# Causal scores in 64-key halves, and value products in two halves of queries, in a gated-attention and FFN kernel

## The chip, the cores and the metric

The kernel runs on one core of one Trainium2 chip. The metric is the device time of one execution in microseconds (us). Before the change the median of three runs is 655.03 us (653.73 to 656.40). The execution that was profiled took 653.01 us; its span, from its first to its last instruction, is 651.2 us.

## The reference, cut to what matters

There are 4 sequences, 8 heads, 768 steps and a head dimension of 48. Per head a complex state is decayed element by element and updated at each step, and only its real part is read:

```
S_re, S_im = a_re*S_re - a_im*S_im + k v^T,  a_re*S_im + a_im*S_re     # |a| capped at 0.999
y[t] = q[t] @ S_re
```

The 8 heads' outputs side by side give x, 3072 x 384. Then h = x @ w_in (384 x 2048), g = h * cos(h), and the result is g @ w_out (2048 x 384). All data is float32 (the weights arrive as float64).

## The kernel before, in words

**Chunks.** Time is cut into chunks of C = 128 steps: 24 chunks n in all, 6 to a sequence, handled in 12 groups g of G = 2 chunks. For a chunk the recurrence becomes a causal attention within the chunk plus a term from the state at its start. With the decay folded into queries and keys, both have 2 x 48 = 96 rows (real and imaginary part).

**Scores.** `f_scores(n, hh)` (line 958) does four heads (HH = 4, hh = 0 or 1): for each a matmul with the 128 keys as weights and the 128 queries as moving columns, contraction over 96 rows, into the PSUM tile `sc`. Then one VectorE multiply by the constant mask `causal` (0.25 on and above the diagonal, 0 below it) moves 128 x 512 numbers into the SBUF tile `atm`. Keys lie on the partitions, so a quarter of each 128 x 128 square (keys 64 to 127 against queries 0 to 63) is computed and then multiplied by 0.

**Values.** `f_out(n)` (line 970) makes the output transposed, dimension by step, in the PSUM tile `yp`. Two heads share a PSUM column block: the even head's 48 rows start at partition 0, the odd head's at partition 64 (`side`). For each pair p of heads it issues the two sides' products of values with `atm` (contraction over 128 keys, weights of 48 columns, 128 moving columns) and, unless the chunk is a sequence's first, the two sides' products of `state` with the queries (contraction over 96 rows, 48 weight columns, 128 moving columns), which add to the same place. ScalarE then copies both halves out.

**State.** `f_state(n)` (tile `sp`) multiplies keys and values for the next chunk's state, except in a sequence's last chunk.

**FFN.** `mm1` (tile `hp`) multiplies x by w_in; ScalarE and VectorE make g of it. From group 2 on the second product is done in seven instead of eight block products (`seventh`, tiles `sum` and `op`, moving 192 columns), issued in half-products of 8 matmul records.

A float32 matmul appears in the trace as two MATMUL records, each with its own LDWEIGHTS: 192 score products are 384 records.

**What sets the order.** All TensorE instructions go through `matmul` (line 687), which chains each one behind the one before. GpSimd's instructions are chained in the same way (`chain(..., "gpsimd")`, lines 549, 629, 1279); VectorE's ordinary ones go through `vector` (line 676) and are ordered by the framework from group 2 on. From there `weave` (line 1213) writes the order: each list of steps is spread over a stretch of the group's unit interval and all are sorted. In group n the `chunks(n)` steps (scores hh = 0, scores hh = 1, state, output, for both chunks) lie in 0.0 to 0.36, between half-products of the group before; the FFN's first product comes from 0.56 on.

**Groups 0 and 1** (chunks 0 to 3) have an order written by hand and use other forms in part (`f_rows` for chunks 0 and 1). PEG = 2 is the first group of the regular kind, so 20 of the 24 chunks are regular.

**GpSimd** does little: it issues the DMAs of constants and raw weights. In groups 4 to 11 `guarded` (line 1281) gives it one tiny copy that waits for a gate tile and then two DMAs of raw weights (tile `raw`, one buffer at that stage), whose exponents VectorE and ScalarE check.

Of the kernel before, what the change touches and what calls it, by code (L numbers as in the profile page):

```python
# [11 lines left out]
F32 = mybir.dt.float32  # L12
# [7 lines left out]
ALU = mybir.AluOpType  # L20
# [467 lines left out]
def fast_path(ctx, tc, q, k, v, a_re, a_im, moe_w_in, moe_w_out, out, least, odd, wide,  # L488
# [7 lines left out]
    nc = tc.nc  # L496
    B, H, S, D = q.shape
    DM, DF = moe_w_in.shape
    C = 128
    NCH = S // C  # L500
    G = 2
    N = B * NCH
    NG = N // G
    D2 = 2 * D
    HH = H // 2
    ND = DM // C
    Q4 = C // 32
# [6 lines left out]
    ld = ctx.enter_context(tc.tile_pool(name="ld", bufs=1))  # L514
    gt = ctx.enter_context(tc.tile_pool(name="gt", bufs=1))
    ft = ctx.enter_context(tc.tile_pool(name="ft", bufs=2))
# [4 lines left out]
    stage = {"pool": room.enter_context(tc.tile_pool(name="stage", bufs=1)), "bufs": 4}  # L521
    pa = ctx.enter_context(tc.tile_pool(name="pa", bufs=5, space=PSUM))
# [3 lines left out]
    causal_np = (step_np[:, None] <= step_np[None, :]).astype(np.float32)  # L526
# [10 lines left out]
    def chain(ins, engine="scalar"):  # L537

        if engine in tail:
            behind(ins, tail[engine])  # L540
        tail[engine] = ins

    def behind(ins, other):
        tc.add_manual_dep(ins.ins, other.ins.name, mybir.DependencyInfo(
            mybir.DependencyClass.NoSync, mybir.DependencyReason.DATA))

    def constant(array, name, queue=None, pool=consts):
        t = pool.tile(list(array.shape), F32, name=name)
        put = (queue or nc.gpsimd).dma_start(
            out=t, in_=nc.inline_tensor(array, name=name + "_const").ap())  # L550
        if queue is None:
            chain(put, "gpsimd")
        return t
# [6 lines left out]
    X = [dict() for _ in range(NG)]  # L560
    Y = [dict() for _ in range(N)]
# [3 lines left out]
    PEG, PER = 2, 1  # L565
# [118 lines left out]
    vector, scalar = Ordered(nc.vector, "vector"), Ordered(nc.scalar, "scalar")  # L684

    def matmul(out, **kw):
        chain(nc.tensor.matmul(out, **kw), "tensor")  # L687
# [156 lines left out]
    def p_even(g, i, n):  # L844
        for _ in even_steps(g, i, n):
            pass
# [8 lines left out]
    def p_apply(g, i, n):  # L855
        x = X[g]
        P, Q, u = (cut(x[name], i, n) for name in ("P", "Q", "mag"))
        vector.tensor_tensor(out=Q, in0=cut(x["k"], i, n), in1=Q, op=ALU.mult)
        vector.tensor_tensor(out=u, in0=cut(x["q"], i, n), in1=P, op=ALU.mult)

    def g_angle(g, i, n):

        at = cut(X[g]["tan"], i, n)
        special(out=at, in_=at, func=AF.Arctan)
# [4 lines left out]
    def g_carry(g):  # L869

        n, some = g * G, ds(C - 32, 32)
        if g >= PEG and n % NCH:
            head = cut(X[g]["tan"], 0, 1)[some]
            X[g]["carried"] = vector.scalar_tensor_tensor(
                out=head, in0=before(n)[some], scalar=carry[some], in1=head,
                op0=ALU.mult, op1=ALU.add)

    def g_split(g):
        if g >= PEG:
            X[g]["split"] = upper_half(g, cut(X[g]["tan"], 0, G), 1.0 / math.pi)()  # L880
# [71 lines left out]
    def queries(n, h):  # L952
        g, i = divmod(n, G)
        if g < PEG:
            return X[g]["qT"][:, i * H + h].rearrange("p q j -> p (q j)")
        return X[g]["qT"][:, :, i * H + h]

    def f_scores(n, hh):
        y = Y[n]
        if hh == 0:  # L960
            y["atm"] = ft.tile([C, H, C], F32, tag="atm", name="atm")
        ps = pa.tile([C, HH, C], F32, tag="a", name="sc")
        for h in range(HH):
            head = hh * HH + h
            matmul(ps[:, h], lhsT=X[n // G]["kT"][:, n % G * H + head],
                   rhs=queries(n, head), start=True, stop=True)
        y["masked"] = vector.tensor_tensor(
            out=y["atm"][:, ts(hh, HH)], in0=ps, in1=causal.unsqueeze(1).to_broadcast([C, HH, C]), op=ALU.mult)

    def f_out(n):  # L970
        y, (g, i) = Y[n], divmod(n, G)
        vals = X[g]["v"][:, i]
        state = y.get("state")
        if i == 0:
            X[g]["yT"] = ft.tile([C, HH, G, C], F32, tag="yT", name="yT", bufs=1)
        ps = pa.tile([C, HH, C], F32, tag="a", name="yp")
        for p in range(HH):
            for side in range(2):
                matmul(ps[ds(side * 64, D), p], lhsT=vals[:, 2 * p + side],
                       rhs=y["atm"][:, 2 * p + side], start=True, stop=(state is None))  # L980
            if state is not None:
                for side in range(2):
                    matmul(ps[ds(side * 64, D), p], lhsT=state[:, 2 * p + side],
                           rhs=queries(n, 2 * p + side), start=False, stop=True)
        for side in range(2):
            half = ds(side * 64, D)
            scalar.copy(out=X[g]["yT"][half, :, i], in_=ps[half])

    def f_rows(n, lo=0, hi=H):

        y, (g, i) = Y[n], divmod(n, G)
        state = y.get("state")
        if lo == 0:
            y["yr"] = pa.tile([C, H, D], F32, tag="a", name="yr")
        ps = y["yr"]
        for h in range(lo, hi):
            matmul(ps[:, h], lhsT=y["atm"][:, h], rhs=X[g]["v"][:, i, h],
                   start=True, stop=(state is None))
            if state is not None:
                matmul(ps[:, h], lhsT=queries(n, h), rhs=state[:, h], start=False, stop=True)  # L1000
        if hi < H:
            return
        y["rows"] = msb.tile([C, DM], F32, tag="ot", name="rows")
        scalar.copy(out=y["rows"], in_=ps.rearrange("p h d -> p (h d)"))
# [74 lines left out]
    def gate_sine(g, jp):  # L1079
        x = X[g]  # L1080
        ps = x["hp"][jp]
        gate = x["gate"][jp] = msb.tile([C, 2, G * C], F32, tag="gate", name="gate", bufs=8)
        junk = msb.tile([C, 2, G * C], BF16, tag="junk", name="junk", bufs=1)
        special(out=gate, in_=ps, func=AF.Sin, scale=1.0 / in_scale, bias=half_pi_b)
        scalar.activation(out=junk, in_=ps, func=AF.Square, scale=1.0 / in_scale,
                          accum_out=wide[:, ds(g * (NJ // 2) + jp, 1)])

    def gate_product(g, jp):
        x = X[g]
        gate = x["gate"][jp]  # L1090
        gated = vector.tensor_tensor(out=gate, in0=x["hp"].pop(jp), in1=gate, op=ALU.mult)
        x.setdefault("gated", gated)

    def mm1_gate(g, jp):
        gate_sine(g, jp)
        gate_product(g, jp)
# [143 lines left out]
    def powers(g):  # L1240
        return [lambda i=i: p_powers(g, i) for i in range(G)]

    def prods(g):
        if not 0 <= g < NG:
            return
        if g not in (1, 2):
            yield from powers(g)
            yield lambda: g_angle(g, 0, G)
        yield lambda: (g_carry(g), g_split(g))
        yield lambda: (p_even(g, 0, G), p_apply(g, 0, G))  # L1250
# [23 lines left out]
    def second(g, i):  # L1274
        return [lambda j0=j0: mm2(g, i, j0, 4) for j0 in range(0, NJ, 4)] if g < PLAIN else []
# [26 lines left out]
    chain(nc.gpsimd.tensor_copy(out=alls, in_=one_b.to_broadcast([C, C])), "gpsimd")  # L1302
    parts = into + back
    pieces = [weight(dst, src) for dst, src in parts[:2]]
    causal = constant(causal_np * np.float32(0.25), "causal")
    pieces += [weight(dst, src) for dst, src in parts[2:RAW]]
    carry = constant(carry_np, "carry")
    chain(nc.gpsimd.tensor_copy(out=exact, in_=ones), "gpsimd")
# [3 lines left out]
    one, two = (log_steps(0, i, 1) for i in range(2))  # L1312
# [93 lines left out]
    state = state_next(1)  # L1406
# [55 lines left out]
    state = state_next(2)  # L1462
# [12 lines left out]
    state = state_next(3)  # L1475
# [86 lines left out]
    Ordered.by_hand, Ordered.mark = (), dict(tail)  # L1562
    for jp in 6, 7:
        mm1_gate(1, jp)
    room.close()
    stage.update(pool=ctx.enter_context(tc.tile_pool(name="late", bufs=1)), bufs=1)
    quarters()
    for n in range(2, NG):
        weave((mixes(n - 1, 2, 4), 0.0, 0.12), (logs(n + 1), 0.0, 0.02), (chunks(n), 0.0, 0.36),
              (upper[2:] if n == 2 else [], 0.0, 0.2), (products(n - 1, 0, 2 + (n < NG - 1)), 0.0, 0.36),  # L1570
              (prods(n + 1), 0.25, 0.27), (second(n - 1, 1), 0.36, 0.5),
              (products(n - 1, 2 + (n < NG - 1), 7), 0.4, 0.56),
              (phases(n + 1), *((0.472, 0.476) if n == PLAIN else (0.516, 0.524))),
              (keys(n + 1), *((0.5, 0.62) if n == PLAIN else (0.53, 0.64))),
              (last_quarter() if n == PLAIN else [], 0.9, 1.0), (first(n), 0.56, 1.0),
              (mixes(n, 0, 2), 0.9, 1.0), (guarded(n - 1, per) if n > 3 else [], 0.1, 0.9))
# [101 lines left out]
```

## Time and profile before

| what | value |
|---|---|
| median of 3 runs | 655.03 us |
| profiled execution | 653.01 us, span 651.2 us, granted TensorE clock 1.000 |
| `sc` MATMUL records | 384, of them 320 in regular chunks |
| `yp` MATMUL records from `atm` / from `state` | 352 / 304 |
| `atm` multiplies on VectorE | 48 x 689 ns |
| GpSimd busy | 30.9 us in 53 instructions |

An engine's busy time counts a stretch once, however many of its instructions overlap there. Since matmuls are pipelined, a group's mean duration (276 ns for `sc`) is not what one more of them costs; the distance from start to start is. In the timeline, consecutive instructions of one form are merged into one row with its count, start and length.

### The profile page before, as it was taken

The numbers are of one execution on the slowest core, as the hardware profiler recorded it, in microseconds if no ns is written. First come the engines' busy times: TensorE is split into PE (matmuls) and PEld (weight loads), VectorE is DVE, ScalarE is ACT, GpSimd is POOL, SyncE is SP. The second block draws the span as 40 slices with busy tenths as digits, with TensorE's granted clock in tenths as the row PEclk, the third lists the DMA queues.
The fourth block names the chain that finished last, engine by engine and source line by source line (L and its number), as shares of the span: only waits on it lengthen the run. The fifth ranks groups of instructions, "written<-read, shape, count | busy, mean of one in ns | idle before, by whom it ended". The sixth has DMA issues, their size and how long they took to land.

```text
span 651.2 us, 10758 instructions
## 1 busy us (share of the span) xinstructions
PE 641.0 (98%) x4075; PEld 576.4 (89%) x4075; DVE 492.0 (76%) x799; ACT 392.8 (60%) x726; POOL 30.9 (5%) x53
## 2 busy tenths in 40 slices
PE   8999999999999999999999999999999999999997
PEld 6888877777999999899899899899899999999996
DVE  6999989888687688786787787876877878862251
ACT  7898687284583593494494485485576476433330
POOL 4010200000000000010010010000000000000000
PEclk9999999999999999999999999999999999999999
DMA  9968755727627656747738737836836843363001
GB/s 249 244 179 203 225 164 123 170 62 182 146 49 182 158 146 148 194 110 167 209 82 191 204 85 167 205 96 151 226 105 146 219 123 98 112 134 120 25 1 31
DMA packets 232920, 94.90 MB, mean 146 GB/s; under 512 B 208701, under 2 KB 221246, under 8 KB 232858
## 3 DMA queue, kind: packets, MB, share of 16 engines
q1 hardware_dynamic: 225320, 68.51, 45.3%
q0 software_dynamic: 5824, 25.50, 11.7%
q8 instruction: 34, 0.56, 0.4%
q10 hardware_dynamic: 1714, 0.11, 0.2%
q14 instruction: 28, 0.23, 0.1%
HBM read 69.28 MB, written 24.81 MB: 144 GB/s over the span
## 4 chain that ended last, share of the span: by engine, by line
PE 92%; ACT 4%; DVE 3%; DMA 0%; issue 0%; SPq 0%; DVEq 0%
PE hp L687 38%; PE op L687 18%; PE sum L687 16%; PE sc L687 6%; PE yp L687 6%; PE sp L687 4%; PE phs L687 2%; PE lgs L687 1%; ACT tan L707 1%; PE yr L687 1%; PE tp L948 1%; ACT rs L707 1%; ACT lg L707 1%; ACT L703 1%; DVE mag L676 1%; DVE atm L676 1%
## 5 line engine op out<-in xcount | busy, mean ns | idle before, releaser
L687 PE MATMUL hp<-xT,w_in 128*128 128x256 f32 (+1 forms) x1176 | 252.5, 375 | 0.0
L687 PEld LDWEIGHTS hp<-xT,w_in 128*128 128x128 f32 x1176 | 219.6, 190 | 30.2 <-issue 0.2
L707 ACT ACTIVATE gate<-hp,half_pi_b 128x512 f32<-128x512 f32 x96 | 66.0, 687 | 118.5 <-PE hp L687 118.5
L687 PE MATMUL op<-w_out,gate 128*128 128x192 f32 (+1 forms) x448 | 100.7, 374 | 0.0
L676 DVE TENSOR_TENSOR gate<-hp,gate 128x512 f32<-128x512 f32 x96 | 65.7, 684 | 45.8 <-ACT junk L676 45.7
L687 PEld LDWEIGHTS op<-w_out,gate 128*128 128x128 f32 x448 | 75.9, 190 | 16.9 <-issue 2.0
L676 ACT ACTIVATE junk<-hp 128x512 bf16<-128x512 f32 x96 | 56.7, 591 | 0.0
L687 PE MATMUL sum<-t_s,s 128*128 128x192 f32 x320 | 56.3, 329 | 0.0
L687 PEld LDWEIGHTS sum<-t_s,s 128*128 128x128 f32 x320 | 52.1, 190 | 1.5 <-issue 1.5
L676 DVE TENSOR_TENSOR atm<-sc,causal 128x512 f32<-128x512 f32 x48 | 32.9, 689 | 23.4 <-PE sc L687 23.4
L687 PEld LDWEIGHTS sc<-qT,kT 96*128 96x128 f32 x384 | 47.4, 192 | 2.3 <-issue 0.6
L687 PE MATMUL sc<-qT,kT 96*128 96x128 f32 x384 | 49.0, 276 | 0.2 <-ACT qT L676 0.2
L676 ACT ACTIVATE ot<-sum 128x192 f32<-128x192 f32 x39 | 12.6, 322 | 53.7 <-PE sum L687 53.4
L676 DVE SCALAR_TENSOR_TENSOR ot<-op,ot 128x192 f32<-128x192 f32 x40 | 13.3, 354 | 38.0 <-PE op L687 36.4
L687 PE MATMUL yp<-atm,v 128*48 128x128 f32 x352 | 33.6, 277 | 0.9 <-ACT Q L707 0.6
L703 ACT ACT_TABLE_LOAD x24 | 30.8, 1283 | 1.2 <-PEq L1662 0.7
L676 ACT COPY yT<-yp 48x512 f32<-48x512 f32 x44 | 25.3, 574 | 7.4 <-PE yp L687 7.0
L687 PE MATMUL yp<-qT,state 96*48 96x128 f32 x304 | 29.7, 272 | 0.0
L687 PE MATMUL sum<-w_out,gate 128*128 128x192 f32 x160 | 29.7, 329 | 0.0
L687 PE MATMUL sp<-v,ks 128*96 128x48 f32 x320 | 29.7, 245 | 0.0
L687 PEld LDWEIGHTS sp<-v,ks 128*96 128x96 f32 x320 | 29.6, 165 | 0.0
L676 ACT CAST tan<-phs 128x384 int32<-128x384 f32 x24 | 11.4, 480 | 29.4 <-PE phs L687 29.4
(147 smaller groups left out, 987.4 us busy)
## 6 DMA issues: line engine op xcount, KB each, us to landing
moved<-tr SPq DMA_DIRECT2D x20, 768.0 KB
raw<-in_moe_w_in_dram POOLq DMA_DIRECT2D x16, 768.0 KB, 5.1
raw<-in_moe_w_out_dram POOLq DMA_DIRECT2D x16, 768.0 KB, 4.6
kT<-moved SPq DMA_DIRECT2D x40, 192.0 KB
qT<-moved SPq DMA_DIRECT2D x10, 768.0 KB
k<-in_k_dram SPq DMA_DIRECT2D x24, 192.0 KB
q<-in_q_dram SPq DMA_DIRECT2D x24, 192.0 KB
v<-in_v_dram SPq DMA_DIRECT2D x24, 192.0 KB
```

The costliest lines, as they stand in the source:

```text
L676: ins = getattr(self.engine, op)(**kw)
L687: chain(nc.tensor.matmul(out, **kw), "tensor")
L703: chain(nc.scalar.preload_act_table_set(table))
L707: chain(nc.scalar.activation(func=func, **kw))
L948: chain(nc.tensor.transpose(ps[:, h], X[g][name[0] + "s"][:, x0 + h].rearrange("p a d -> p (a d)"), ident), "tensor")
```

## The change: what it does

In chunks 4 to 23 `f_scores` becomes `half_scores` and the products with `atm` in `f_out` become `half_out`; a new `swap_values` serves them.

- `half_scores` cuts the keys into two halves of 64, so that the weights have 64 columns. The first half is multiplied with all 128 queries, the second only with queries 64 to 127. The even head's first half goes to partitions 0 to 63, the odd head's to 64 to 127; the second halves go to the opposite side. A pair of heads thus fills three blocks of 64 columns instead of four, with four products instead of two, and the mask multiply moves 128 x 384 instead of 128 x 512.
- `half_out` issues the state products first, then the values in two halves of queries: for queries 0 to 63 only the 64 first keys count, so the contraction is over 64 rows (partitions 0 to 63 for the even head, 64 to 127 for the odd one); for queries 64 to 127 it is over 128. Each has 64 moving columns.
- In the odd head's last block the key halves lie swapped, so its values must too: `swap_values` makes, with two GpSimd copies per group, a tile `odd` of the odd heads' values with halves of partitions exchanged. It has one buffer and is issued in the weave of the group before, at 0.4 to 0.42.
- A mask `halves_mask` is loaded as one more constant; `causal` and part of the first groups' `atm` move to a pool that is released later.

```diff
+    def swap_values(g):
+        odd_v = X[g]["odd"] = ld.tile([C, G, HH, D], F32, tag="odd", name="odd_v", bufs=1)
+        for lo in 0, C // 2:
+            src = X[g]["v"][ds(C // 2 - lo, C // 2)].rearrange("p g (x two) d -> p g x two d", two=2)
+            chain(nc.gpsimd.tensor_copy(out=odd_v[ds(lo, C // 2)], in_=src[:, :, :, 1]), "gpsimd")
+    def half_scores(n, hh):
+        y, (g, i), S = Y[n], divmod(n, G), C // 2
+        if hh == 0:
+            y["atm"] = ft.tile([C, HH, 3, S], F32, tag="atm", name="atm")
+        ps = pa.tile([C, HH // 2, 3, S], F32, tag="a", name="sc")
+        keys = X[g]["kT"].rearrange("d x q j -> d x (q j)")
+        for p in range(HH // 2):
+            heads = [i * H + hh * HH + 2 * p + side for side in range(2)]
+            for side, head in enumerate(heads):
+                matmul(ps[ds(side * S, S), p, ds(0, 2, 1 + side)], lhsT=keys[:, head, 0:S],
+                       rhs=X[g]["qT"][:, :, head], start=True, stop=True)
+            for side, head in (1, heads[1]), (0, heads[0]):
+                matmul(ps[ds((1 - side) * S, S), p, 1 + side], lhsT=keys[:, head, S:C],
+                       rhs=X[g]["qT"][:, Q4 // 2:Q4, head], start=True, stop=True)
+        y["masked"] = vector.tensor_tensor(
+            out=y["atm"][:, ts(hh, HH // 2)], in0=ps,
+            in1=halves_mask.unsqueeze(1).to_broadcast([C, HH // 2, 3, S]), op=ALU.mult)
+    def half_out(n, ps):
+        y, (g, i), S = Y[n], divmod(n, G), C // 2
+        state = y.get("state")
+        for p in range(HH):
+            vals = X[g]["v"][:, i, 2 * p], X[g]["odd"][:, i, p]
+            if state is not None:
+                for side in range(2):
+                    matmul(ps[ds(side * 64, D), p], lhsT=state[:, 2 * p + side],
+                           rhs=queries(n, 2 * p + side), start=True, stop=False,
+                           skip_group_check=True)
+            for half in range(2):
+                for side in range(2):
+                    rows = ds(0, C) if half else ds(side * S, S)
+                    matmul(ps[ds(side * 64, D), p, ts(half, S)], lhsT=vals[side][rows],
+                           rhs=y["atm"][rows, p, half * (1 + side)], start=(state is None),
+                           stop=True, skip_group_check=True)
     def f_scores(n, hh):
+        if n >= PEG * G:
+            return half_scores(n, hh)
...
-        for p in range(HH):
+        if g >= PEG:
+            half_out(n, ps)
+        for p in range(HH if g < PEG else 0):
...
-    causal = constant(causal_np * np.float32(0.25), "causal")
+    causal = constant(causal_np * np.float32(0.25), "causal", pool=stage["pool"])
+    S = C // 2
+    halves_np = np.stack([np.tile(causal_np[:S, :S], (2, 1)), causal_np[:, S:],
+                          np.roll(causal_np[:, S:], S, axis=0)], axis=1) * np.float32(0.25)
+    halves_mask = constant(halves_np, "halves_mask")
...
+    swap_values(PEG)
...
+              ([lambda: swap_values(n + 1)] if n + 1 < NG else [], 0.4, 0.42), (second(n - 1, 1), 0.36, 0.5),
```

More of the change, by code (lines that the diff above doesn't have):

```diff
@@ L958, in f_scores @@
     def f_scores(n, hh):
+        if n >= PEG * G:
+            return half_scores(n, hh)
         y = Y[n]
-        if hh == 0:
-            y["atm"] = ft.tile([C, H, C], F32, tag="atm", name="atm")
+        pool = stage["pool"] if hh else ft
+        atm = pool.tile([C, HH, C], F32, tag="atm", name="atm", bufs=2)
+        y.setdefault("atm", []).append(atm)
         ps = pa.tile([C, HH, C], F32, tag="a", name="sc")
@@ L967, in f_scores @@
         y["masked"] = vector.tensor_tensor(
-            out=y["atm"][:, ts(hh, HH)], in0=ps, in1=causal.unsqueeze(1).to_broadcast([C, HH, C]), op=ALU.mult)
+            out=atm, in0=ps, in1=causal.unsqueeze(1).to_broadcast([C, HH, C]), op=ALU.mult)
     def f_out(n):
@@ L976, in f_out @@
         ps = pa.tile([C, HH, C], F32, tag="a", name="yp")
-        for p in range(HH):
+        if g >= PEG:
+            half_out(n, ps)
+        for p in range(HH if g < PEG else 0):
             for side in range(2):
                 matmul(ps[ds(side * 64, D), p], lhsT=vals[:, 2 * p + side],
-                       rhs=y["atm"][:, 2 * p + side], start=True, stop=(state is None))
+                       rhs=y["atm"][p // 2][:, p % 2 * 2 + side], start=True, stop=(state is None))
             if state is not None:
@@ L996, in f_rows @@
         for h in range(lo, hi):
-            matmul(ps[:, h], lhsT=y["atm"][:, h], rhs=X[g]["v"][:, i, h],
+            matmul(ps[:, h], lhsT=y["atm"][h // HH][:, h % HH], rhs=X[g]["v"][:, i, h],
                    start=True, stop=(state is None))
@@ L1570, in fast_path @@
               (upper[2:] if n == 2 else [], 0.0, 0.2), (products(n - 1, 0, 2 + (n < NG - 1)), 0.0, 0.36),
-              (prods(n + 1), 0.25, 0.27), (second(n - 1, 1), 0.36, 0.5),
+              (prods(n + 1), 0.25, 0.27),
+              ([lambda: swap_values(n + 1)] if n + 1 < NG else [], 0.4, 0.42), (second(n - 1, 1), 0.36, 0.5),
               (products(n - 1, 2 + (n < NG - 1), 7), 0.4, 0.56),
```

## Prediction

> **What bounds the kernel now.** I read the page's busy shares first, then the chain that ended last, then TensorE's timeline for one group.
>
> ```profile
> PE 641.0 (98%) x4075; PEld 576.4 (89%) x4075; DVE 492.0 (76%) x799; ACT 392.8 (60%) x726; POOL 30.9 (5%) x53
> ...
> PE 92%; ACT 4%; DVE 3%; DMA 0%; issue 0%; SPq 0%; DVEq 0%
> ```
>
> TensorE is busy in 98% of the span and makes 92% of the chain. In the regular part it hardly idles: the table by stretches shows 51.00 us busy of 51.00 between 204 and 255 us. So what the change adds to or takes from TensorE's start-to-start distances goes into the time one for one, and what it takes from VectorE does not count. The timeline of the group that starts near 276 us (columns: start us, length, engine, line, form, records) gives the prices.
>
> ```profile
> 276.09 1.06 PE L687 MATMUL sc<-qT,kT 96*128 96x128 f32 x8
> 276.98 1.47 PE L687 MATMUL sum<-w_out,gate 128*128 128x192 f32 x8
> 278.28 1.06 PE L687 MATMUL sc<-qT,kT 96*128 96x128 f32 x8
> 279.18 1.48 PE L687 MATMUL sp<-v,ks 128*96 128x48 f32 x16
> 280.50 1.53 PE L687 MATMUL sum<-w_out,gate 128*128 128x192 f32 x8
> ...
> 283.32 0.39 PE L687 MATMUL yp<-atm,v 128*48 128x128 f32 x4
> 283.54 0.39 PE L687 MATMUL yp<-qT,state 96*48 96x128 f32 x4
> 283.86 1.57 PE L687 MATMUL op<-w_out,gate 128*128 128x192 f32 x8
> 285.26 1.95 PE L687 MATMUL sc<-qT,kT 96*128 96x128 f32 x16
> ```
>
> Starts matter, not lengths. A score record costs (276.98 - 276.09) / 8 = 0.111 us; a 192-column record (278.28 - 276.98) / 8 = 0.1625, or 0.85 ns a moving column. An `sp` record, with only 48 moving columns but 96 weight columns, costs (280.50 - 279.18) / 16 = 0.0825, or 0.86 ns a weight column. A `yp` record costs 0.22 / 4 = 0.055: half a score record's, with as many moving columns. So the two sides of `yp` (48 weight columns at partition 0, 48 at partition 64) already run at once, 0.11 us for two.
>
> The same timeline, opened a little later, shows what entering and leaving this two-sided form costs.
>
> ```profile
> 281.70 0.33 PE L687 MATMUL sum<-w_out,gate 128*128 128x192 f32 x1
> 281.96 0.43 PE L687 MATMUL yp<-atm,v 128*48 128x128 f32 x4
> 282.21 0.39 PE L687 MATMUL yp<-qT,state 96*48 96x128 f32 x4
> 282.44 0.39 PE L687 MATMUL yp<-atm,v 128*48 128x128 f32 x4
> ```
>
> Entering: from the last `sum` to the first `yp` 0.26 us pass instead of 0.16, and the first four `yp` take 0.25 instead of 0.22: 0.10 + 0.03 = **0.13 us**. Leaving (fence before): 283.54 to 283.86 is 0.32 instead of 0.22, and the eight `op` take 1.40 instead of 1.30: 0.10 + 0.10 = **0.20 us**. I read the first term of each as the array running empty, the second as a weight load that nothing covers (0.03 for 48 columns, 0.10 for 128). The full-array forms follow one another without it: from `sc` to `sum` nothing is lost.
>
> **The change part by part.**
>
> *Scores, per pair of heads.* Removed: 4 records at 0.111 = 0.445 us. Added: two two-sided steps with 128 moving columns at 0.11 and two with 64. The trace has no record of 64 moving and 64 weight columns. By the rates above its stream takes 64 x 0.85 = 0.054 and its weights 64 x 0.86 = 0.055, so I take 0.055 a step; the upper bound is 0.11, no gain from fewer columns. That is 0.33, a saving of 0.115 us, or 9.2 us over 2 pairs x 2 calls x 20 chunks (lower end: nothing).
>
> *Scores, round trips.* Each run of scores must now enter and leave the two-sided form. In the regular groups TensorE's sequence is `sc` x8, half-product, `sc` x8, `sp`, half-product, `yp`, half-product, `sc` x16, half-product, ..., `yp`: three runs of scores a group. Groups 2 to 9 have 3, group 10 has 4, and group 11 has 2 of its own and one that follows `yp` directly and so costs no trip: 24 + 4 + 2 = 30. With 64 weight columns I put entering at 0.10 + 0.04 and leaving at 0.20, 0.34 together: 10.2 us (bounds: nothing, as between `sc` and `sum`, and 0.40, two leavings). Scores thus come to **+1.0 us**.
>
> *Values, streaming.* A chunk with state now takes 16 steps of 0.11 = 1.76 us. After: 8 state steps at 0.11 and 16 half steps at 0.055 = 1.76. No gain, since `yp` was already two-sided; at the upper bound of 0.11 a half step, +0.88 a chunk or 17.6 us.
>
> *Values, changes of row count.* For each pair of heads the contraction goes 96 rows (state), 64 rows at partitions 0 or 64 (first half), 128 rows (second half), then 96 again. The trace shows 128 to 96 and back within `yp` at no cost. It shows no 64-row matmul. From below the price is nothing, as between 128 and 96; I see no gain. From above it is a leaving, 0.20. I take 0.13, an entering with weights of 48 columns, because the step from full rows to half the rows is nearest to the one change of array shape that the trace has. Per chunk with state there are 2 x 4 = 8; in the three regular chunks that open a sequence (6, 12, 18) 7, the first entering being paid already: 17 x 8 + 3 x 7 = 157, x 0.13 = **20.4 us**.
>
> A rule speaks on this step. The Trainium skill, "TensorEngine Tiling (Array Packing)", Key Properties, says that switching the tiling mode, not just the tile, drains the engine, and lists 64-row and 128-row tiles as different modes. By the rule each of the 157 changes empties the array, and the sum is +21.4 us with the entering's 0.13 as the price; by the row of 128 against 96 rows it is +1.0 us. The same page's Overview promises up to twice the speed where the contraction or the weights have 64 or less; the 0.055 us of `yp` says that the two sides already have that factor, and the 64-row halves add no third and fourth tile.
>
> *VectorE.* 40 mask multiplies go from 128 x 512 to 128 x 384:
>
> ```profile
> L676 DVE TENSOR_TENSOR atm<-sc,causal 128x512 f32<-128x512 f32 x48 | 32.9, 689 | 23.4 <-PE sc L687 23.4
> L676 DVE TENSOR_TENSOR tan<-phs,tan 128x384 f32<-128x384 f32 x24 | 13.3, 557 | 5.7 <-ACT tan L676 4.5
> ```
>
> 689 - 557 = 132 ns x 40 = 5.3 us less VectorE work, worth nothing: VectorE waits for `sc`, and TensorE waited for `atm` 0.3 us in all.
>
> *GpSimd.* 20 copies of 384 elements; the nearest row, a 128 x 128 cast at 0.42 to 0.45 us, makes each some 1.3 us, 26 us on an engine that is 5% busy. But the first copy of a group must wait until the group before has finished its last `yp` (one buffer), here 291.5 us, and behind it in GpSimd's chain stands a raw-weight DMA that now starts at 279.13. The check that reads it is on VectorE, where two gate multiplies and phases could be late. The framework orders VectorE after what it knows of this, so I take nothing; if the check stays early, VectorE stalls in 8 groups, at some 2.5 us of TensorE each (one `hp` tile) 20 us. The extra constant adds one issue of 0.55 us ahead of the raw weights in the start: 0 to 0.55, taken as nothing.
>
> *Sum:* 1.0 + 0 + 20.4 = +21.4 us. 653.0 + 21.4 = 674.4 for the profiled execution; the median lies 2.0 above it, so **676.5 us**. A measurement of this kernel tells about 0.5%, 3.3 us, from no change.
>
> **The rivals.**
>
> 1. *Changing from 96 to 64 rows is free.* For: 128 to 96 is. Against: 64 rows at partition 64 is another part of the array, not fewer rows of the same. Time: 655.0 + 1.0 = 656, no difference.
> 2. *Faster: the round trips of scores are hidden too.* Mechanism: with half-width weights the next load is taken while the array still runs, so that `sc` enters as it does today. Then 9.2 us are saved: 655.0 - 9.2 = 645.8. It decides only if a round trip costs under 9.2 / 30 = 0.31 us and a row change under 9.2 / 157 = 0.06. Against: each of the entries and exits of `yp` in the trace shows the 0.10.
> 3. *Issue-bound.* TensorE's sequencer may not feed a matmul and its load every 0.028 us; the densest the trace shows over a stretch is 0.055. Then half steps cost 0.11: scores +10.2, values +17.6 + 20.4, together 703. Against: queued work can be fed while the array runs empty.
> 4. *Row changes at half the price* (0.07): 655.0 + 1.0 + 11 = 667.
>
> **How the numbers follow.** My forecast (667 to 688) 0.64; rival 1 0.16; rival 2 0.05; rival 3 or the GpSimd stall 0.08; rival 4 (660 to 667) 0.07. Rival 1 counts as within 0.5%, but for 0.01 on its fast side; so faster 0.06, same 0.15, slower 0.79. The range 656 to 688 takes the forecast, rival 4 and the upper half of rival 1: 0.79.
>
> **What would show it.** Right: in the timeline each `yp` chunk (1.76 us plus entry and exit) grows by about 1 us, with gaps of some 0.1 us at each change to and from 64 rows; `sc` x16 of one call takes some 0.66 us instead of 0.89, with 0.3 us lost around it; granted clock stays 1.00. Wrong: `yp` keeps its length (rival 1), `sc` joins `op` without a gap (rival 2), half steps start 0.11 apart (rival 3), or VectorE waits for `raw` with `hp` late behind it.

## The result and the profile after

The changed kernel takes 693.41 us (median of four, 692.19 to 696.7) against 654.38 us for the kernel before in the same comparison: a ratio of 1.0604, 95% interval 1.0554 to 1.0654, or **39 us more**. The profiled execution took 692.19 us, span 690.4, granted clock 0.997. The forecast was +21.4 us; the direction was right, the size was not.

The page after, its busy times and then its chain by engine:

```profile
PE 668.3 (97%) x4715; PEld 572.6 (83%) x4715; DVE 489.5 (71%) x799; ACT 391.5 (57%) x726; POOL 46.8 (7%) x74
...
PE 69%; DMA 12%; DVE 6%; ACT 6%; issue 4%; SPq 3%; POOL 0%; DVEq 0%; POOLq 0%; ACTq 0%
```

Two things differ from before, and they are two different losses. TensorE is busy for 27.3 us more (668.3 against 641.0) and idle for 11.9 us more (690.4 - 668.3 = 22.1 against 651.2 - 641.0 = 10.2). And TensorE's share of the chain fell from 92% to 69%, with DMA at 12% where before it had none. "97% busy" would not have told it: the chain does.

**The longer products.** TensorE's timeline of one `yp` chunk after (start us, length, engine, line, form, records):

```profile
463.93 0.43 PE L687 MATMUL yp<-qT,state 96*48 96x128 f32 x4
464.29 0.25 PE L687 MATMUL yp<-atm,v 64*48 64x64 f32 x1
...
464.38 0.22 PE L687 MATMUL yp<-atm,v 64*48 64x64 f32 x1
...
464.53 0.26 PE L687 MATMUL yp<-atm,v 128*48 128x64 f32 x1
...
464.63 0.22 PE L687 MATMUL yp<-atm,v 128*48 128x64 f32 x1
...
464.68 0.39 PE L687 MATMUL yp<-qT,state 96*48 96x128 f32 x4
465.00 0.25 PE L687 MATMUL yp<-atm,v 64*48 64x64 f32 x1
...
466.93 2.87 PE L687 MATMUL sum<-t_s,s 128*128 128x192 f32 x16
```

Only the `v` side is shown; the `odd_v` side starts within 0.01 us of it, so the two 64-row tiles do run at once. From one state product to the next short step 0.32 us pass (464.68 to 465.00) where four records need 0.22: 0.10 lost. From the first to the second short step it is 0.09, where a short step in a row takes 0.05 to 0.06 (experiment 6 below): some 0.04 lost. So 0.14 for the change from 96 to 64 rows, and likewise from 64 to 128 rows (464.38 to 464.53 is 0.15, then 0.10 to the next: 0.10 and 0.04 to 0.05 lost). From 128 back to 96 rows 0.05 pass: nothing lost. The chunk takes 3.00 us (463.93 to 466.93) instead of 1.90.

The weight loads (PEld) of the same chunk show where the 0.10 us lie:

```profile
464.29 0.12 PEld L687 LDWEIGHTS yp<-atm,v 64*48 64x48 f32 x1 [0.18 <-issue]
...
464.63 0.19 PEld L687 LDWEIGHTS yp<-qT,state 96*48 96x48 f32 x4
```

At the change to 64 rows the load starts no earlier than its product (464.29 both), after 0.18 us without a load; at the change back to 96 rows it starts 0.05 ahead of its product (464.63 against 464.68).

**The new waits.** The waits of the kernel after (waiting engine and tile, releaser, us in total, times, longest):

```profile
POOL odd_v L963 <- PE yp L687: 159.0, 8, 48.3
...
DVE raw L676 <- DMA raw<-in_moe_w_out_dram: 20.9, 7, 4.2
DVE raw L676 <- DMA raw<-in_moe_w_in_dram: 13.7, 5, 4.2
...
PE hp L687 <- DVE gate L676: 8.0, 5, 2.4
```

GpSimd's wait for `yp` is harmless by itself, as GpSimd is nearly idle. But VectorE now waits 34.6 us for raw weights (5.4 before), and TensorE then 8.0 us in `hp` for VectorE's gate multiplies, which it never did before. With its other new waits (1.8 us in `hp` for the check of `raw`, 1.7 for `qT`, 0.8 for `xT`) that is 12.3 us. The path from one to the other is in the chain of waits of the kernel after around one such place (start us, length, what):

```profile
476.03 6.26 DMA raw<-in_moe_w_out_dram
...
482.31 0.57 DVE raw L676
...
490.66 0.61 DVE gate L676
491.32 14.90 PE hp L687 x60
```

A DMA issued at 476.03 lands at 482.3; VectorE checks it; the phase work and a long transpose that stand behind the check in VectorE's order follow; then comes the gate multiply for which `hp` has waited 2.31 us. Why the DMA is late is on GpSimd's own timeline, first of the kernel after, then of experiment 1 below, which has the swap at another place:

```profile
451.68 0.36 POOL L1328 COPY after<-gate 1x1 f32<-1x1 f32 x1 [29.46 <-DVE gate L676]
467.16 1.86 POOL L963 COPY odd_v<-v 64x384 f32<-64x384 f32 x2 [15.12 <-PE yp L687]
468.97 0.71 POOL L629 DMA_DIRECT2D raw<-in_moe_w_out_dram  x1
476.03 0.72 POOL L629 DMA_DIRECT2D raw<-in_moe_w_out_dram  x1 [6.36 <-ACT ot L676]
```

```profile
443.62 0.37 POOL L1328 COPY after<-gate 1x1 f32<-1x1 f32 x1 [35.61 <-DVE gate L676]
444.16 0.71 POOL L629 DMA_DIRECT2D raw<-in_moe_w_out_dram  x1 [0.17 <-issue]
454.64 0.72 POOL L629 DMA_DIRECT2D raw<-in_moe_w_out_dram  x1 [9.77 <-ACT raw L676]
459.13 1.85 POOL L963 COPY odd_v<-v 64x384 f32<-64x384 f32 x2 [3.77 <-PE yp L687]
```

In the kernel after the first raw-weight DMA leaves 17.3 us after the gate copy (451.68 to 468.97), since the two swap copies ahead of it in GpSimd's queue wait 15.12 us for the last `yp` of the group before to free their buffer. With the copies behind both DMAs it leaves 0.54 us after it, and the second one 11.0 us after it (443.62 to 454.64) instead of 24.4 (451.68 to 476.03).

### The profile page after: what moved, and what is told of

The parts are those of the page before. It is cut to its first block, busy times and chain, and to the rows that moved or that the text cites. A ratio compares the mean times of both kernels' runs of the same rounds, so it can differ in the third digit from the quotient of the medians.

```text
span 690.4 us, 12092 instructions
## 1 busy us (share of the span) xinstructions
PE 668.3 (97%) x4715; PEld 572.6 (83%) x4715; DVE 489.5 (71%) x799; ACT 391.5 (57%) x726; POOL 46.8 (7%) x74
## 4 chain that ended last, share of the span: by engine, by line
PE 69%; DMA 12%; DVE 6%; ACT 6%; issue 4%; SPq 3%; POOL 0%; DVEq 0%; POOLq 0%; ACTq 0%
PE hp L687 26%; PE op L687 11%; PE sum L687 9%; PE yp L687 8%; PE sc L687 6%; DMA raw<-in_moe_w_out_dram 4%; PE sp L687 4%; DMA qT<-moved 2%; SPq L936 1%; DMA x<-yT 1%; DVE ks L676 1%; PE lgs L687 1%; DVE qs L676 1%; DMA k<-in_k_dram 1%; PE phs L687 1%
## 5 line engine op out<-in xcount | busy, mean ns | idle before, releaser
L687 PE MATMUL hp<-xT,w_in 128*128 128x256 f32 (+1 forms) x1176 | 256.5, 378 | 11.2 <-DVE gate L676 8.0
L687 PEld LDWEIGHTS hp<-xT,w_in 128*128 128x128 f32 x1176 | 219.8, 191 | 45.7 <-DVE gate L676 11.1
L676 DVE TENSOR_TENSOR atm<-sc,halves_mask 128x384 f32<-128x384 f32 x40 | 22.2, 555 | 38.6 <-PE sc L687 38.1
L687 PE MATMUL yp<-atm,v 64*48 64x64 f32 (+2 forms) x352 | 47.3, 240 | 0.0
L676 ACT ACTIVATE raw<-raw,least_e_b 128x768 f32<-128x768 uint32 x16 | 16.1, 1009 | 54.5 <-DVE raw L676 54.5
L687 PEld LDWEIGHTS sc<-qT,kT 96*64 96x64 f32 (+1 forms) x704 | 36.9, 142 | 11.6 <-issue 10.1
L687 PEld LDWEIGHTS yp<-atm,v 128*48 128x48 f32 (+1 forms) x352 | 27.8, 119 | 20.3 <-issue 12.3
L687 PE MATMUL yp<-atm,odd_v 64*48 64x64 f32 (+1 forms) x320 | 44.1, 236 | 0.0
L687 PE MATMUL sc<-qT,kT 96*64 96x128 f32 (+2 forms) x704 | 41.6, 254 | 2.3 <-DMA qT<-moved 1.7
L676 DVE TENSOR_SCALAR raw<-raw 128x768 uint32<-128x768 uint32 x16 | 9.0, 560 | 34.5 <-DMA raw<-in_moe_w_out_dram 20.9
```

The costliest lines, as they stand in the source:

```text
L676: ins = getattr(self.engine, op)(**kw)
```

## The experiments

My theory after the result: about half of the 39 us is the row changes, as forecast, and the other half the GpSimd queue. The rivals: the row changes cost twice what I took; or the scores' round trips do; or the swap's price is its work or its pressure on the memory and not its place in the queue.

**1. The swap copies put behind the raw-weight DMAs,** nothing else edited (VectorE's order shifts a little, since the framework places its work anew):

```diff
-              ([lambda: swap_values(n + 1)] if n + 1 < NG else [], 0.4, 0.42), ...
+              ([lambda: swap_values(n + 1)] if n + 1 < NG else [], 0.79, 0.81), ...
```

> The changed kernel with one position moved: the copies of the odd heads' values are issued at 0.79 to 0.81 of the group instead of 0.40 to 0.42, so that in GpSimd's chain they stand behind the two raw-weight DMAs instead of ahead of them; TensorE's instructions are the same. Theory A (of the 39 us, some 21 are changes of row count and some 17 are late raw weights, because the copies wait for the group's last yp and the DMAs queue behind them): about 676 us, VectorE no longer waits for raw with hp late behind it. Rival B (all 39 us lie in TensorE's own stream, or come from the copies themselves): 690 to 694 us.

Measured: 674.44 us, 1.0292 (1.0274 to 1.0309). The same copies in another place give back 19.0 us. TensorE no longer waits for a gate multiply; it is idle for 672.6 - 663.4 = 9.2 us, less than before the change. Of the 17.8 us between the two spans, 12.9 are idle time and 4.9 busy time (668.3 against 663.4); 4.0 of the latter stand in the row of the `hp` products (256.5 against 252.5), some 1.7 of them are the clock, told of at the end, and the rest I have not told apart.

**2. All halves over 128 rows,** with the swap where the change has it:

```diff
-                    rows = ds(0, C) if half else ds(side * S, S)
+                    rows = ds(0, C)
```

> The changed kernel, but the products for queries 0 to 63 contract over all 128 rows, so that no product has 64 rows; this changes the computation (a pair's two heads are mixed for these queries). The number of instructions stays. Theory A (157 changes of row count at 0.13 us = 20.4 us, the raw-weight wait stays): 673 us, and a yp chunk with state takes 1.76 us and entry and exit. Rival B (no stall, each change costs 0.25): 655 us. Rival C (changes are free, the half steps are what is slow): 693 us.

Measured: 674.05 us, 1.0283 (1.0266 to 1.03). No change of row count is left, and 19.4 us are gone: in size the other half. The wait of `hp` for a gate multiply stays (9.1 us).

**3. The scores alone,** from the kernel before: `half_scores` as in the change, values in one product of 128 queries, no swap.

```diff
+            for side in range(2):
+                matmul(ps[ds(side * 64, D), p], lhsT=vals[side],
+                       rhs=y["atm"][:, p, ds(0, 2, 1 + side)], start=(state is None),
```

> The scores' part alone: half_scores and its mask as in the changed kernel, the values as one product of 128 queries over all 128 rows, from v without the swap (this changes the computation: the blocks that two heads share are not told apart, and the odd heads' halves are not exchanged). No GpSimd copies, no 64-row products. Theory A (streaming saves 9.2 us, 30 round trips of 0.34 cost 10.2): 654.4 + 1.0 = 655.4 us. Rival B (the scores pay for part of the loss): 660 us or more. Rival C (the round trips are hidden): 646 us.

Measured: 654.78 us, 0.9999 (0.9986 to 1.0011). The scores' saving and whatever their round trips cost cancel.

**4. The values alone,** from the kernel before: whole scores, the values' products in halves of 64 and 128 rows, no swap.

```diff
+                    rows = ds(0, C if half else S)
+                    matmul(ps[ds(side * 64, D), p, ts(half, S)], lhsT=vals[side][rows],
+                           rhs=y["atm"][p // 2][rows, p % 2 * 2 + side, ts(half, S)], ...
```

> The values' part alone: scores and mask as before the change, values in two halves of queries with 64 rows (both heads at partitions 0 to 63) and 128 rows, no swap. The same result as the reference's computation. Theory A (157 changes of row count at 0.13, half steps no gain): 654.4 + 20.4 = 675 us. Rival B (the values' part makes all of the loss by itself): 690 us or more.

Measured: 673.46 us, 1.0296 (1.0261 to 1.0332). The three parts add up: +0.1 for the scores, +18.8 for the values, +19.0 for the swap's place (after less experiment 1) make 37.9 of the 39.0 us. So they hardly interact. TensorE's timeline of this run has 3.00 us for a `yp` chunk with state, as the kernel after has, though here both heads' 64 rows lie on the same partitions: the number of rows makes the cost, and not their place.

**5. A wait of the same kind alone.** The kernel before with one copy of a single number on GpSimd, at the place where the swap stands, which waits for the group before:

```diff
+              ([lambda: wait_for(X[n]["yT"][0:1, 0, 1, 0:1])] if n + 1 < NG else [], 0.4, 0.42), ...
```

> The kernel before with one thing added: where the changed kernel issues its copies (0.40 to 0.42 of the group), GpSimd gets one copy of a single number of the group's last output tile, so that its chain waits for about the same moment, ahead of the raw-weight DMAs. TensorE's instructions are those of before. Theory A (the queue behind a waiting GpSimd instruction is what cost 17 us): 668 to 674 us, VectorE waits for raw, hp late behind it. Rival B (the wait costs only together with the longer yp or the copies): 654 to 657 us.

Measured: 677.31 us, 1.0353 (1.033 to 1.0376): 22.9 us from a copy of one number, more than I expected. GpSimd's timeline of this run, then TensorE's waits:

```profile
299.76 0.57 POOL L1279 COPY after<-yT 1x1 f32<-1x1 f32 x1 [14.73 <-ACT yT L676]
300.27 0.74 POOL L629 DMA_DIRECT2D raw<-in_moe_w_in_dram  x1
```

```profile
PE hp L687 <- DVE gate L676: 8.2, 5, 2.6
PE sc L687 <- DMA qT<-moved: 3.7, 4, 1.7
PE hp L687 <- DMA xT<-x: 3.5, 2, 1.9
```

The wait of 14.73 us ahead of the DMA and the 8.2 us in `hp` are nearly those of the change (15.12 and 8.0). The swap's work and its memory traffic are thus not needed for the loss: a wait ahead of the DMA in GpSimd's queue makes it. The two further rows are 4.7 us longer than in the kernel after (1.7 and 0.8 there), which would cover the excess of 3.9 us over 19.0; this copy waits for `yT`, which is made from `yp` and so comes later. No run takes the excess apart.

**6. Row changes grouped.** The swap late as in 1, and in `half_out` first the state products of all pairs, then the halves with 128 rows, then those with 64, so that a chunk has one change of rows instead of seven or eight:

```diff
+        for half in 1, 0:
+            for p in range(HH):
...
+                    add(p, side, ts(half, S), vals[side][rows], y["atm"][rows, p, half * (1 + side)])
```

> The changed kernel with the copies at 0.79 to 0.81, and in each chunk all products of one row count together: state for all pairs, then queries 64 to 127, then queries 0 to 63, so that a chunk changes its row count once instead of 7 or 8 times. Same instructions, same result. Theory A (137 of 157 changes go, 0.13 us each = 17.8): 674.4 - 17.8 = 656.6 us. Rival B (64-row products are slow in themselves): 670 to 674 us.

Measured: 657.03 us, 1.005 (1.0031 to 1.0069). The timeline of a chunk in this run, the `v` side:

```profile
436.96 1.08 PE L687 MATMUL yp<-qT,state 96*48 96x128 f32 x16
437.87 0.22 PE L687 MATMUL yp<-atm,v 128*48 128x64 f32 x1
...
438.26 0.22 PE L687 MATMUL yp<-atm,v 128*48 128x64 f32 x1
...
438.42 0.25 PE L687 MATMUL yp<-atm,v 64*48 64x64 f32 x1
...
438.51 0.22 PE L687 MATMUL yp<-atm,v 64*48 64x64 f32 x1
...
439.00 0.43 PE L687 MATMUL op<-w_out,gate 128*128 128x192 f32 x1
```

State to 128 rows: no loss. Seven short steps from 437.87 to 438.26, 0.056 each. The one change, 438.26 to 438.42 and on to 438.51, is 0.25 instead of 0.11: 0.14. The chunk takes 2.04 us, 0.14 over the 1.90 of before. The loss belongs to each change of rows, and not to the products.

**7 and 8. The scores of both chunks in one run,** and the first chunk's output straight behind them, so that the scores need no round trip of their own, where they had three a group; 7 on top of 6, and 8 the same order in the kernel before, as its control:

```diff
+        def opening():
+            for n in range(g * G, g * G + G):
+                for hh in range(2):
+                    f_scores(n, hh)
+            f_out(g * G)
```

> As the kernel with rows grouped, and the order of a group changed: all four score calls together and the first chunk's output straight behind them, so that the scores need no entry and exit of their own. Theory A (30 round trips of 0.34 us = 10.2 go): 656.6 - 10.2 = 646 us, below the kernel before. Rival B (the masks come late when four score tiles follow one another, or PSUM's five buffers run out): a wait of about 1 us in each of 10 groups, 656 us.

> A control: the kernel before with that same order of a group and nothing else. Its scores use the full array and have no round trip to save. Theory A: no difference, 653 to 656 us. Rival B (the order itself is worth something): outside of that.

Measured: 664.96 us, 1.017 (1.0136 to 1.0203), and 665.0 us, 1.0179 (1.0154 to 1.0204). Both miss theory A. The order costs the kernel before as much, about 11 us; so it says nothing on the round trips. TensorE's waits of 7 name the place, and those of 8 have the same row with 7.5 us in 5 waits:

```profile
PE hp L687 <- DMA xT<-x: 9.8, 5, 3.5
```

The transposed output `xT` comes too late for the `hp` of the same group. The weave hands out due times by the steps of a group; with six steps instead of ten the second chunk's output lies ahead of the log step's products (`lgs`) and no longer behind them. In SyncE's queue of run 7 the issue of `x` (459.17 us) stands straight behind that of `row` (458.88), which waits for the log step. I took this for the cause; the next experiments try it.

**9, 9b and 10. The log step earlier,** on top of 7 (two places) and, as a control, of 8:

```diff
-              (prods(n + 1), 0.25, 0.27),
+              (prods(n + 1), 0.19, 0.21),
```

(9b: 0.13, 0.15.)

> As the kernel with one run of scores, but the next group's lgs products and what hangs on them (positions 0.25 to 0.27) are issued at 0.19 to 0.21, ahead of the second chunk's output as they stand in the kernel before. Theory A (in the one-run order hp waits 9.8 us for xT, because in SyncE's queue x stands behind the row that comes out of lgs; without that the 30 round trips show their worth): 646 to 649 us. Rival B (the order costs something else as well, or the trips are not worth 10 us): 655 us or more.

> The same with lgs one half-product earlier still (0.13 to 0.15). Theory A: 646 to 649 us, as little waiting as with 0.19 or less. Rival B: lgs waits for VectorE's lo there, so 650 us or more.

> The control to them: the kernel before with one run of scores and lgs at 0.19 to 0.21. Theory A (the order costs nothing once x is not late, and with full-array scores it saves nothing): 653 to 656 us. Rival B (the order gains by itself): under 652 us.

Measured: 665.08 us, 1.0139 (1.0117 to 1.0161); 702.73 us, 1.072 (1.0697 to 1.0743); and 662.85 us, 1.0104 (1.008 to 1.0127). All three miss theory A. In 9 the wait for `xT` fell from 9.8 to 0.8 us, and `lgs` waits 10.7 us in its place: 6.7 for VectorE's `lo` and 4.0 for ScalarE's `hi`, its operands, which are not made yet. In 9b these two waits grow to 29.6 us, and the mean granted clock is 0.971; in the control they are 5.6 us.

**11. `x` moved ahead of `row` and the loads in SyncE's queue,** on top of 7:

```diff
+        if g > PEG:
+            behind(put, late["x"])
```

> The kernel with one run of scores per group (rows grouped, copies at 0.79 to 0.81), in which hp waited 9.8 us for xT and 1.8 for VectorE: now SyncE's queue has x and xT ahead of the next group's row and of the loads of k, q and v. lgs stays behind the second chunk's output. Theory A (the waits were the queue's, and the saved round trips show once they are gone): 665.0 - 11.6 = 653 us or somewhat less, down to 646 us if nothing else waits, so 646 to 653; against the kernel before with 654 to 656. Rival B (x itself, or lgs and what hangs on it, is late in this order): 656 us or more.

Measured: 681.61 us, 1.0392 (1.0363 to 1.0422). It misses theory A: the wait for `xT` stayed (11.1 us), so the place of `x` behind `row` is not what makes it late, and the cause stays open. `yp` now waits 10.6 us for VectorE (5.4 for the state, 5.2 for the masks), whose order the framework made anew.

**12 and 13. Only the second chunk's scores moved,** straight behind the first chunk's output, on top of 6, with the 64-row halves first, then the 128-row ones, then the state; so scores follow a form with 48 or 64 weight columns, and a group has two round trips instead of three, with all else at its due time. 13 is the same order in the kernel before.

```diff
+            yield lambda: (f_out(a), f_scores(b, 0), f_scores(b, 1))
```

> The kernel with rows grouped and copies at 0.79 to 0.81 (657.0 us), with the second chunk's scores straight behind the first chunk's output instead of one half-product later, and in each output the 64-row products first, then 128 rows, then state, so that output and scores follow one another in one form. Theory A (a round trip costs 0.34 us): 10 of them less, 657.0 - 3.4 = 653.6 us, within 0.5% of the kernel before. Rival B (round trips cost nothing in time): 657 us. Rival C (the order brings a wait): over 658 us.

> The control: the kernel before with the second chunk's scores straight behind the first chunk's output, nothing else. Its yp leaves the two-sided form either way. Theory A: no difference, 654 to 656 us. Rival C (the order brings a wait): over 658 us.

Measured: 654.11 us, 0.9987 (0.9967 to 1.0007), and 656.04 us, 1.0019 (1.0005 to 1.0034). Relative to experiment 6 experiment 12 is some 4 us less (0.0063 x 654.4, uncertain by about 2) for ten round trips saved, where 0.34 us each gives 3.4; the order of the products within a chunk changed with it. This version comes back to the time of before, and does not beat it.

## Why the prediction was wrong

**The step that failed** is GpSimd's: "The framework orders VectorE after what it knows of this, so I take nothing". The term that was put at nothing cost 19.0 us (after less experiment 1), and a wait of this kind alone costs the kernel before 22.9 (experiment 5). Everything needed stood in the prediction itself: the copy waits for the last `yp` of the group before, the raw-weight DMA stands behind it, "if the check stays early, VectorE stalls in 8 groups", 20 us. I gave that case, with rival 3, a chance of 0.08, on nothing but an assumption on how VectorE's order would come out, which no row of the profile supports. VectorE's check of `raw` was not moved behind the gate multiplies: VectorE waited 34.6 us for weights, and `hp` 8.0 us for VectorE. With this term at its own price the sum is 21.4 + 20 = +41.4 us, near the +39.0 measured. That is luck in part: the 20 us stood for eight stalls of one `hp` tile each, and the profile shows five waits for a gate multiply, of 8.0 us together, with 4.3 us of other waits and 4.9 of longer busy time beside them. The copies' own work, estimated at 26 us, was less (GpSimd's busy time grew by 15.9 us), and experiment 1, which keeps it, lies within 1 us of the sum of experiments 3 and 4.

**Row changes:** taken at 157 x 0.13 = 20.4 us; the values alone measured +18.8 (experiment 4), all rows -19.4 (experiment 2). That is 0.12 a change; the timeline shows 0.14, 21.6 us over the 20 chunks, and the difference of some 2 us is not explained. Right in size, and in mechanism as far as the rows show it. Rival 1 (free) and rival 4 (half the price) fall: a chunk grew by 1.10 us, and grouping the changes took most of it away. The rule cited in the prediction (the Trainium skill, "TensorEngine Tiling (Array Packing)", Key Properties: a change of tiling mode drains the engine) fits: I read the 0.14 us as about 0.10 of empty array and 0.04 of weight load that nothing covers. The page names no price. Its list of modes has 128, 64 and 32 rows and says nothing of 96; that 96 and 128 rows go together is shown by this case alone (0.05 us from the one to the other).

**Scores:** taken at +1.0 us, a saving of 9.2 and round trips of 10.2. Measured +0.1, interval -0.9 to +0.7 (experiment 3). The single terms are seen in the timelines, first of experiment 7, where four calls follow one another, then of the kernel after:

```profile
437.45 2.90 PE L687 MATMUL sc<-qT,kT 96*64 96x128 f32 x64
440.18 1.04 PE L687 MATMUL yp<-qT,state 96*48 96x128 f32 x16
```

```profile
506.15 0.89 PE L687 MATMUL sc<-qT,kT 96*64 96x128 f32 x16
506.97 1.57 PE L687 MATMUL sum<-w_out,gate 128*128 128x192 f32 x8
508.47 0.89 PE L687 MATMUL sc<-qT,kT 96*64 96x128 f32 x16
```

Four calls in a row take 2.73 us, 0.68 each instead of 0.89: a saving of 0.21 x 40 = 8.4 us, where 9.2 was taken. A call by itself takes 0.82, and the half-product behind it takes 1.50 to the next scores instead of 1.30: 0.14 + 0.20 = 0.34 for the round trip, as taken. Thirty of these would be 10.2 and the sum +1.8, about 1 us above the interval; by the total of experiment 3 a round trip is (8.4 + 0.1) / 30 = 0.28. Experiments 6 and 12 put it at about 0.4 (4 us for ten), uncertain by 0.2. Rival 2 (hidden round trips, 645.8 us) falls with experiment 3.

**Values' streaming,** taken at nothing: right, the short steps are not issue-bound, so rival 3's 0.11 us a step falls. **VectorE's 5.3 us,** taken as worth nothing: nothing speaks against it, since experiment 3, which has these shorter masks, gained nothing; it was not tried alone.

**What stays open:** whether one run of scores a group could be made to pay. Experiments 7, 9, 9b and 11 each brought another wait (for `xT`, for the log step's operands, for the masks), so the round trips were never alone there, and why `xT` is late in that order was not found; and the exact split of the 22.9 us in experiment 5 between its three waits.

## What to carry to other kernels

Before an instruction that waits is put on an idle engine, read what stands behind it in that engine's queue and follow it to its reader, and to what stands behind the reader: an engine that is 5% busy held up TensorE, which was 98% busy, because a DMA issue stood behind its wait. A case that can be priced from the profile must not be set to nothing because a scheduler may avoid it; either its order is read from a trace, or part of the price goes into the sum. And cutting a product in half by rows saved nothing here, where two half-width tiles already ran at once, while each change of row count cost 0.14 us: group all products of one row count ahead of the next.

## What the runs showed of the hardware

**A wait of 2 us can cost more than its length.** After one of the new waits TensorE's granted clock falls. The table by stretches of the kernel after, behind the wait of 2.31 us that ends at 491.3 us, and then that behind the wait of 2.42 us that ends at 325.8 (stretch, its us, then busy us and instructions of PE, PEld, DVE, ACT, POOL, the granted clock, DMA share, GB/s):

```profile
491.30:494.00 2.70, 2.68 (x7) 2.12 (x8) 2.67 (x2) 0.00 (x0) 0.00 (x0) 0.54 0.70 291
494.00:497.00 3.00, 3.00 (x14) 2.55 (x13) 2.12 (x5) 1.04 (x2) 0.00 (x0) 0.85 0.96 299
```

```profile
325.80:328.50 2.70, 2.66 (x12) 2.20 (x12) 2.70 (x2) 0.00 (x0) 0.00 (x0) 1.00 0.70 291
```

After the one, 7 records in 2.70 us; after the other, a wait as long, 12. From 497 us on the clock is 1.00 again. The lower clock took 2.70 x 0.46 + 3.00 x 0.15 = 1.7 us. Of the four waits of over 1 us for a gate multiply in this execution (2.42, 1.28, 2.31, 1.59 us) only the third shows it. In run 9 two gaps of 0.79 and 0.68 us with one record between them were followed by a mean clock of 0.57 from 292 to 296 us. So the length of a wait alone doesn't tell whether the clock falls.

The Trainium skill, "TensorE: Matmul & The Clock Gate", Part 1, describes the throttled state as half the clock, taken after at least one idle window of about 3.4 us, in windows that run freely beside the kernel. The half agrees with the 0.54, and windows that run freely would fit that one of two equal waits was hit; but the wait that was hit lasted 2.3 us, less than the window named there. On that the measurement decides.
